# Pooled attention with a gated-convolution FFN on one core: the schedule rewritten, with q in 96 rows, exp in token order and crossbar transposes from batch 2 on

## The chip, the core and the metric

The kernel runs on one core of one Trainium2 chip. The metric is the time of one execution on the device, in microseconds (us). Before the change the median of three runs is 202.54 us (201.12 to 206.23).

## The reference

Eight batches of attention over pooled keys feed an FFN with a gated convolution. Inputs and output are fp32; the kernel computes in bf16 with fp32 sums.

```python
# q, k, v: 8 batches x 8 heads x 576 tokens x 64
k_p = k.reshape(B, H, 72, 8, D).mean(axis=3)         # 576 keys -> 72
v_p = v.reshape(B, H, 72, 8, D).mean(axis=3)
attn = softmax(q @ k_p.T / 8) @ v_p
x = attn.transpose(0, 2, 1, 3).reshape(B, 576, 512)  # tokens x (heads * 64)
h = relu(x @ w_in)                                   # 512 -> 1024
conv_out[s] = sum_k conv_w[k] * h[s + k - 1]         # 3 taps along the tokens, per channel
out = (h * sigmoid(conv_out)) @ w_out                # 1024 -> 512
```

## The kernel before

All five engines work on one program, whose operations are listed with `pl.add` (name, engine or choice of engines, a planned duration, a function that issues it, what it reads and writes). `Planner.order` (L172) turns the list into one order: a list simulation over planned durations, in which `PARAMS["prio"]` breaks ties; `PARAMS["act"]` says which of the operations that could go to DVE or ACT go to ACT. PSUM is cut into three slots of two banks (A) and two of one bank (B). Where the simulation sees PE idle in the first 60 us, `warm` (L379) puts in filler matmuls of 128 columns of zeros (L388).

Attention goes batch by batch, one or two batches ahead of the FFN.

- *Loads.* POOL issues them and casts fp32 to bf16: k (L447, L451) and v (L467 to L479) as 576 rows of eight tokens, w_in in one DMA of 1 MB (L485), w_out in two (L492). q of batches 0 to 4 comes as 72 rows of eight tokens, all heads (L424); q of batches 5 to 7 token by token in five DMAs a batch, whose pieces are the 64 values of one token and head (L412). `PARAMS["rg"]`, "DDDDDTTT", chooses. POOL also makes the scaled identities for the convolution (L571).
- *Keys and values.* DVE adds the eight tokens of each row (L605, L612, L622, and L654 for v). The key sums are transposed on PE and copied into kz (L642), the value sums are spread into blocks (L658, L663).
- *q.* For batches 0 to 4 a copy brings the heads of a token side by side (`regroup`, L432), PE transposes them (L688) and DVE or ACT copies the result to qT (L694). For batches 5 to 7 SP's queue transposes q by DMA, in the crossbar (L676).
- *Scores and values.* L717 and L719 multiply with the keys (the rest of 16 keys of each pair of heads goes through four strips of 32 columns of the array, L719). One exp on ACT covers 128 keys and 576 tokens (L725); it reads and writes rows of 576 without gaps. L742 and L746 multiply with the values, DVE divides by the sum (L755, L759). Batches 0 to 4 carry the tokens of a tile in the order of q's rows, eight apart.
- *x.* For batches 0 to 4 PE transposes each tile of 128 tokens with a permutation in place of the identity, which puts the tokens in order (L779), and a copy takes it to xT (L785). For batches 5 to 7 SP's queue transposes it (L772).
- *FFN.* w_in times xT (L822; for batch 0 in parts of 384 and 192 tokens, L799), relu on ACT (L828, L806). The convolution is either three matmuls with scaled identities on PE (L945) with the gate on ACT out of PSUM (L952), or off PE: two scaled copies on ACT (L868) or DVE (L870), two additions on DVE (L877, L887), and the gate on ACT (L895). A gate is Tanh, which DVE finishes (L923), or Sigmoid, according to `PARAMS["sw"]`; each change between the two, and back to exp, loads a table on ACT. DVE multiplies h by the gate (L933). w_out takes two batches at a time in nine tiles of 128 tokens (L976), a copy on ACT or DVE takes the result out (L999), and SP's queue stores it (L1004) from three buffers.

Of the kernel before, what the change touches and what calls it, by code (L numbers as in the profile page):

```python
# [15 lines left out]
    "prio": (  # L17
# [84 lines left out]


TINY = 1e-20


class Op:
    __slots__ = ("i", "name", "eng", "dur", "lat", "deps", "prio", "fn", "take", "give", "dma", "width", "done", "users", "after", "kind", "unit", "mode")


class Planner:

# [59 lines left out]
    def order(self):  # L172
# [4 lines left out]
        for o in ops:  # L177
# [3 lines left out]
            for d in o.deps:  # L181
                ops[d].users.append(o.i)
# [919 lines left out]
```

## Time and profile before

| | |
|---|---|
| runs of the kernel (us) | 202.54 median, 201.12 to 206.23 |
| profiled execution, its span (us) | 205.9 |
| instructions | 4566 |
| PE busy, at its end a matmul of L976 | 194.9 us |
| the group with most time on PE | L976, 282 matmuls, 65.4 us |
| the next | L822, 448 matmuls, 60.0 us |
| moved by DMA | 30.02 MB in 52330 packets |

The profiled execution is one execution, on the long side of the three runs; its span is counted from the first instruction to the last. An engine's busy time says nothing of when it was busy, so the page's row of forty slices (busy tenths) and a table of busy time by windows stand beside it. Fillers count as busy PE time. A row such as "L725 ACT ACTIVATE attnT<-psfA x40: 628/657/701, 14.7 to 155.9" gives line, engine, tiles, count, least, median and greatest time of one in ns, and when the first and the last ran. In a row by distance from start to start ("99.04 1.72 ACT ...") the first number is the start and the second the time of one instruction or of a run of like ones. A DMA row gives its KB and the median from issue to landing.

### The profile page before, as it was taken

How to read it: one execution, taken by the hardware profiler on the slowest of the kernel's cores; microseconds unless marked ns; L12 is line 12 of the kernel's file. 1: busy time of each engine (PE TensorE's matmuls, PEld its weight loads, DVE VectorE, ACT ScalarE, POOL GpSimd, SP SyncE). 2: the span in 40 equal slices, each digit the busy share in tenths (PEclk: the TensorE clock that was granted, in tenths of full speed). 3: DMA queues.
4: the chain of work that ended last, by engine and by line, in shares of the span. 5: the costliest groups of instructions: out<-in, count | busy, mean ns of one | idle time of the engine just before them, and what ended most of it. 6: DMA issues, size and time to landing. Idle time of an engine off the chain costs nothing.

```text
span 205.9 us, 4566 instructions
## 1 busy us (share of the span) xinstructions
PE 194.9 (95%) x1770; PEld 133.0 (65%) x1770; DVE 173.3 (84%) x396; ACT 165.3 (80%) x275; POOL 57.0 (28%) x90
## 2 busy tenths in 40 slices
PE   6999999999999999999999999669999999999992
PEld 6978775977557776567755775226756765765541
DVE  3598599999999999999999996893897999778522
ACT  2045799999999999999999999494899867979610
POOL 7999497160223276215412000000000000000000
PEclk9999999999999999999999999996999999999999
DMA  3999999999999999999999999772122625004334
GB/s 32 192 202 205 196 200 200 201 184 192 157 193 238 171 125 173 181 147 158 193 137 167 152 103 151 115 203 105 20 57 41 229 78 155 13 0 168 126 117 154
DMA packets 52330, 30.02 MB, mean 146 GB/s; under 512 B 33468, under 2 KB 47316, under 8 KB 52308
## 3 DMA queue, kind: packets, MB, share of 16 engines
q0 software_dynamic: 32384, 16.73, 71.8%
q1 hardware_dynamic: 19924, 12.99, 30.5%
q8 instruction: 14, 0.23, 0.6%
q14 instruction: 8, 0.07, 0.2%
HBM read 33.44 MB, written 9.44 MB: 208 GB/s over the span
## 4 chain that ended last, share of the span: by engine, by line
PE 38%; DMA 26%; ACT 16%; DVE 12%; issue 3%; POOL 3%; SPq 0%; POOLq 0%; DVEq 0%; ACTq 0%
PE psfB L976 14%; DMA v_b<-in_v_dram 13%; PE psfA L822 12%; DMA q_b<-in_q_dram 6%; DMA qT<-q 6%; ACT tg L895 4%; PE pswA L388 3%; ACT attnT L725 3%; PE psfA L742 2%; ACT hT L828 2%; ACT cv L868 2%; PE psfA L945 2%; DVE p L605 2%; DVE cv L870 1%; DMA xT<-xx 1%
## 5 line engine op out<-in xcount | busy, mean ns | idle before, releaser
L976 PE MATMUL psfB<-w_out,gT 128*128 128x512 bf16 (+1 forms) x282 | 65.4, 378 | 0.0
L822 PE MATMUL psfA<-xT,w_in 128*128 128x288 bf16 x448 | 60.0, 291 | 2.2 <-DMA xT<-xx 2.2
L822 PEld LDWEIGHTS <-w_in 128*128 128x128 bf16 x448 | 43.9, 100 | 16.2 <-DMA xT<-xx 2.4
L976 PEld LDWEIGHTS <-gT 128*128 128x128 bf16 x290 | 27.3, 98 | 28.9
L828 ACT ACTIVATE hT<-psfA 128x576 bf16<-128x576 f32 x56 | 35.1, 656 | 8.4 <-PE psfA L822 8.2
L870 DVE TENSOR_SCALAR cv<-hT,cr 128x576 bf16<-128x576 bf16 x75 | 26.3, 378 | 5.6 <-ACT hT L828 5.4
L933 DVE TENSOR_TENSOR gT<-tg,hT 128x1152 bf16<-128x1152 bf16 x32 | 23.6, 749 | 3.9 <-ACT tg L895 2.0
L759 DVE TENSOR_TENSOR xx<-psfA,rr 128x512 bf16<-128x512 f32 (+1 forms) x40 | 26.5, 679 | 0.2
L868 ACT ACTIVATE cv<-hT,cr 128x576 bf16<-128x576 bf16 x33 | 25.1, 776 | 0.4 <-DVE cv L887 0.2
L725 ACT ACTIVATE attnT<-psfA 128x576 bf16<-128x576 f32 x40 | 24.5, 661 | 0.7 <-PE psfA L717 0.5
L895 ACT ACTIVATE tg<-cv,cn 128x576 bf16<-128x576 bf16 x30 | 22.5, 780 | 0.0
L877 DVE TENSOR_TENSOR cv<-cv,hT 128x1152 bf16<-128x1152 bf16 (+1 forms) x31 | 20.9, 676 | 0.3
L887 DVE TENSOR_TENSOR cv<-cv 128x1152 bf16<-128x1152 bf16 (+1 forms) x31 | 20.8, 674 | 0.2
L999 ACT COPY osb<-psfB 128x512 f32<-128x512 f32 x24 | 14.1, 587 | 6.4 <-PE psfB L976 6.3
L412 POOL DMA_DIRECT2D q<-in_q_dram x15 | 12.8, 863 | 20.1 <-DMA qT<-q 11.3
L895 ACT ACTIVATE tg<-cv,cs 128x576 bf16<-128x576 bf16 x24 | 18.2, 772 | 0.2
L388 PEld LDWEIGHTS <-zero 128*128 128x128 bf16 x239 | 16.1, 108 | 2.8 <-DVE zero L497 2.0
L742 PE MATMUL psfA<-vblk,attnT 128*128 128x130 bf16 (+1 forms) x160 | 15.6, 222 | 2.1 <-DVE xx L759 2.0
L742 PEld LDWEIGHTS <-attnT 128*128 128x128 bf16 (+1 forms) x160 | 11.1, 100 | 5.7 <-DVE xx L759 2.9
L388 PE MATMUL pswA<-zero 128*128 128x128 bf16 x150 | 11.5, 249 | 2.0 <-DVE zero L497 2.0
L717 PE MATMUL psfA<-qT,kz 128*128 128x512 bf16 x64 | 12.4, 286 | 0.3
L746 PE MATMUL psfA<-vblk,attnT 128*128 128x130 bf16 (+1 forms) x80 | 11.2, 221 | 0.0
(92 smaller groups left out, 256.6 us busy)
## 6 DMA issues: line engine op xcount, KB each, us to landing
out_dram<-osb SPq DMA_DIRECT2D x14, 512.0 KB, 4.2
k_b<-in_k_dram POOLq DMA_DIRECT2D x8, 512.0 KB, 13.5
v_b<-in_v_dram POOLq DMA_DIRECT2D x7, 512.0 KB, 13.0
q_b<-in_q_dram POOLq DMA_DIRECT2D x4, 576.0 KB, 15.6
out_dram<-osb SPq DMA_DIRECT2D x7, 256.0 KB, 2.2
q<-in_q_dram POOLq DMA_DIRECT2D x12, 128.0 KB, 15.9
w_in<-in_moe_w_in_dram POOLq DMA_DIRECT2D x1, 1024.0 KB, 10.4
w_out<-in_moe_w_out_dram POOLq DMA_DIRECT2D x2, 512.0 KB, 12.5
```

What stands on the lines that cost most here:

```text
L388: nc.tensor.matmul(out=t, lhsT=zero[:, 0:P], rhs=zero[:, 0:P], start=True, stop=True)
L725: nc.scalar.activation(out=attnT[m][:, t, :], in_=slot(key).rearrange("p i x -> p (i x)")[:, 0:S], func=ACT.Exp, scale=1.0 / 64.0)
L742: nc.tensor.matmul(out=a[0:n, g, c * w:(c + 2) * w], lhsT=attnT[m][:, s, u0:u0 + n], rhs=vblk[m][:, 2 * s:2 * s + 2, :].rearrange("p x d - ...
L759: nc.vector.tensor_tensor(out=xx[i3][0:n].rearrange("p (g h e) -> p g h e", g=2, h=4), in0=av_view()[:, :, :, 0:D], in1=rr[i3][0:n].rearra ...
L822: nc.tensor.matmul(out=t[:, i, 0:HC], lhsT=w_in[:, c, f * P:(f + 1) * P], rhs=xT[m][:, c, i * HC:(i + 1) * HC], start=(c == 0), stop=(c == ...
L828: nc.scalar.activation(out=h_(b)[:, f, hs(b), 2:S + 2].rearrange("p (i x) -> p i x", i=2), in_=slot(key)[:, :, 0:HC], func=ACT.Relu)
L868: nc.scalar.activation(out=cv[y][:, kk // 2, z0:z1, :], in_=src, func=ACT.Copy, scale=sc)
L870: nc.vector.tensor_scalar(out=cv[y][:, kk // 2, z0:z1, :], in0=src, scalar1=sc, scalar2=None, op0=OP.mult)
L877: nc.vector.tensor_tensor(out=cv[y][:, 0, 0:n, :], in0=cv[y][:, 0, 0:n, :], in1=h_at(2), op=OP.add)
L895: nc.scalar.activation(out=tg[i3][:, zs[z0]:zs[z0] + z1 - z0, :], in_=cv[y][:, 0, z0:z1, :], func=ACT.Tanh if half else ACT.Sigmoid, scale ...
L933: nc.vector.tensor_tensor(out=o_, in0=tg[i3], in1=h2, op=OP.mult)
L976: nc.tensor.matmul(out=a[:, 0, j0:j1], lhsT=g[:, c, t * P:(t + 1) * P], rhs=w_out[:, c, j0:j1], start=(c == 0), stop=(c == n_fb - 1), skip ...
```

## The change

The kernel is written anew around the same computation. What differs:

- *Order.* The planner's simulation is gone. `PARAMS["order"]` lists all operations in their order, with the PSUM slot of each and the number of fillers ahead of it ("36A0/77@B0": 36 fillers in A0, then operation 77 into B0). 159 fillers are left of 239, nine of them behind the first matmul with w_in.
- *q.* All batches come as 96 rows of six tokens (pieces of 384 values); batch 0 in parts of 64 and 32 rows. For batches 0 to 5 PE transposes each head by itself, straight from the loaded rows, two heads into the two halves of the output's rows; there is no regroup. Batches 6 and 7 are regrouped and go through the crossbar in two DMAs each.
- *exp.* It writes tokens in order, and to do so it reads PSUM in steps of 96 values. The permutation matrices go; L664 transposes x with the plain identity.
- *x.* 27 of 40 tiles go through the crossbar (batch 2's tiles 2 to 4, batch 3's 1 to 4, all of batches 4 to 7), 13 through PE.
- *w_in.* Half of its rows of its first 512 columns come as fp32 words on SP's queue into a buffer and are converted on ACT (`wc2.0` and `wc2.1`); the other half, and the columns from 512, come in two DMAs by POOL. In POOL's order both stand behind q of batch 1.
- *Pooling* adds in place; for v of batch 5 eight matmuls with the identity do it on PE.
- *Placement.* The scaled identities move from POOL to ACT (13) and DVE (5). Scaled copies: 42 on ACT, 66 on DVE. Ten units of the convolution are on PE (batch 0's f 0 to 3, 5 and 7; one of batch 1, two of batch 2, one of batch 4), the others off it. All gates are Tanh. All output copies are on ACT.

The core of the diff (the new kernel's lines are named by its own numbers in the text):

```diff
 def load_q(b, prio):                                  # after: L245, L250
-    nc.gpsimd.dma_start(out=q_rows(b % NQ)[0:n, t].rearrange("p (h d) -> p h d", d=D), in_=q[b, :, P * t:P * t + n].rearrange("h p d -> p h d"))
...
-    nc.gpsimd.dma_start(out=q_b[b % NQ][r0:r1].rearrange("p h i d -> p h (i d)"), in_=rows_q(b)[r0:r1])
+    nc.gpsimd.dma_start(out=q_b[b % NQ], in_=q[b].rearrange("h (p i) d -> p h (i d)", i=TQ))
...
 def attn_q(b):                                        # after: L550, L557, L571
-    nc.tensor.transpose(out=t[:, 0, (j - j0) * PR:(j - j0 + 1) * PR], in_=q2[b % NQ][0:PR, i, 2 * c:2 * c + 2, :].rearrange("p h d -> p (h d)"),
-                        identity=ident[0:PR, 0:PR])
+    i, c = divmod(8 * g + j, CH)
+    for z in range(2):
+        nc.tensor.transpose(out=t[64 * z:64 * z + 64, 0, j * PQ:(j + 1) * PQ], in_=q_b[b % NQ][:, 2 * c + z, i * D:(i + 1) * D], identity=ident[0:PQ, 0:PQ])
...
+    nc.sync.dma_start(out=flat_out[:, 1152 * j:1152 * j + 1152].rearrange("p (g r) -> p g r", r=PQ), in_=flat_in[:, 1536 * j:1536 * j + 1536], transpose=True)
...
 def attn_s(b, t):                                     # after: L607, L615
-    nc.scalar.activation(out=attnT[m][:, t, :], in_=slot(key).rearrange("p i x -> p (i x)")[:, 0:S], func=ACT.Exp, scale=1.0 / 64.0)
+    nc.scalar.activation(out=at(m)[:, t, :].rearrange("p (r i j) -> p r i j", i=2, j=3),
+                         in_=slot(key)[:, :, 0:HC].rearrange("p i (j r) -> p r i j", j=3), func=ACT.Exp, scale=1.0 / 64.0)
...
 def attn_av(b, t):                                    # after: L664, L668, L673
-    nc.tensor.transpose(out=a[:, 0, c * P:c * P + n], in_=xx[i3][0:n, c * P:(c + 1) * P], identity=(ident[0:n, 0:n] if tr else perm4 if last else perm))
+    nc.tensor.transpose(out=a[:, 0, c * P:(c + 1) * P], in_=xx[i3][:, c * P:(c + 1) * P], identity=ident)
...
 def weights_in():                                     # after: L295, L299, L306, L311
-    nc.gpsimd.dma_start(out=w_in, in_=moe_w_in.rearrange("(c p) f -> p c f", p=P))
+    nc.sync.dma_start(out=wf[:, 0:c1], in_=src[:, 0:c1, 0:512])
+    copy_on(e)(out=w_in[:, c, 0:512], in_=wf[:, c, :])
+    nc.gpsimd.dma_start(out=w_in[:, 2:4, 0:512], in_=src[:, 2:4, 0:512])
+    nc.gpsimd.dma_start(out=w_in[:, :, 512:1024], in_=src[:, :, 512:1024])
...
 def attn_v(b):                                        # after: L434, batch 5 alone
+    nc.tensor.matmul(out=view(), lhsT=ident, rhs=src[:, :, i * D:(i + 1) * D], start=i == 0, stop=i == 7)
...
 def consts():                                         # after: L389, L391
-    nc.gpsimd.tensor_scalar(out=dw[f][:, kk, :], in0=ident, scalar1=s, scalar2=1.0, op0=OP.mult, op1=OP.mult)
+    nc.scalar.activation(out=dw[f][:, kk, :], in_=ident, func=ACT.Copy, scale=s)      # or DVE
```

More of the change, by code (lines that the diff above doesn't have):

```diff
@@ L136, in add @@
         o.eng = eng if isinstance(eng, dict) else {eng: dur}
-        if len(o.eng) > 1 and self.on_act is not None:
-            e = "ACT" if name in self.on_act else "DVE"
-            o.eng = {e: o.eng[e]}
-        o.lat = lat
-        o.fn, o.prio, o.take, o.give, o.dma = fn, prio + self.shift.get(name, 0.0), take, give, dma and dma[:2]
-        o.width = dma[2] if dma and len(dma) > 2 else 4
+        o.lat, o.fn, o.take, o.give, o.dma, o.tile = lat, fn, take, give, dma, tile
         deps = set()
@@ L286, in packets @@
-def packets(n, nbytes, cast=True, engines=16):
-    return n / engines, 0.003 + 0.0000785 * nbytes if cast else 0.004 + 0.000034 * nbytes, engines // 4
+        out, seen = [], set()
+        for x in PARAMS["order"].split():
+            warm = None
+            if "/" in x:
+                w, x = x.split("/")
+                warm = (int(w[:-2]), w[-2:])
+            mode = x.endswith("s")
+            x, _, slot = x.rstrip("s").partition("@")
+            o = self.ops[int(x)]
+            o.mode = mode
+            assert o.i not in seen and seen.issuperset(o.deps) and (o.after is None or o.after in seen), o.name
+            seen.add(o.i)
+            if slot:
+                self.held[o.take] = (slot[0], int(slot[1]))
+            e = next(iter(o.eng)) if len(o.eng) == 1 else "ACT" if o.name in self.on_act else "DVE"
+            out.append((e, o, warm))
@@ L430, in regroup @@
+    def regroup(b, x):
         for h in range(0, H, 4):
             def fn(e, h=h):
-                copy_on(e)(out=q2[b % NQ][0:PR, :, h:h + 4, :], in_=q_b[b % NQ][:, h:h + 4].rearrange("p h i d -> p i h d"))
-            pl.add(f"qg.{b}.{h}", {"DVE": 0.6, "ACT": 1.8}, 0, fn, reads=[("ql", b % NQ, 0), ("ql", b % NQ, 1)],
-                   writes=[("q", b % NQ, h + z) for z in range(4)] + ([("qt", b % NQ)] if h else []), prio=pr + 0.01 * h,
-                   free=[("qn", b % NQ, t) for t in range(NT)])
@@ new lines, in load_v, with fn @@
+        if b == 0:
+            for c in range(4):
+                def fn(e, c=c):
+                    nc.gpsimd.dma_start(out=v_b[m][32 * c + 16:32 * c + 32, 4, :], in_=src[P:P + 16, c, :])
+                pl.add(f"ldv{b}.t{c}", "POOL", 0.5, fn, reads=[("vz", m)], writes=[("v", m, 2 + c)], dma=(16, 0.087, 16))
+            return
+        def fn(e):
+            nc.gpsimd.dma_start(out=v_b[m][:, 4, :], in_=src[P - 16:P + 16, :, :].rearrange("y c e -> c y e"))
+        pl.add(f"ldv{b}.t", "POOL", 0.7, fn, reads=[("vz", m)], writes=[("v", m, 2 + c) for c in range(4)], dma=(P, 0.087, 4))
@@ L518, in consts @@
-        pl.add("perm1", "DVE", 0.15, fn, reads=["ident"], writes=[("perm", 1)], prio=-47)
-        def fn(e):
-            t = slot(("cw",))
-            nc.tensor.transpose(out=t[:, 0, 0:24], in_=cw_raw, identity=identf)
-        pl.add("cwT", "PE", 0.1, fn, reads=["cwr", "identf"], writes=["cwp"], prio=-46, take=("cw",))
+            nc.tensor.transpose(out=slot(("cw",))[:, 0, 0:24], in_=cw_raw, identity=identf)
+        pl.add("cwT", "PE", 0.1, fn, reads=["cwr", "identf"], writes=["cwp"], take=("cw",), tile=3)
@@ new lines, in by_identity, with view, fn, attn_k @@
+    def by_identity(b, x, src, reads):
+        key = ("pm", b, x)
+        def view():
+            return slot(key)[:, 0, 0:NT * D].rearrange("p (t d) -> p t d", d=D)
+        def fn(e):
+            for i in range(8):
+                nc.tensor.matmul(out=view(), lhsT=ident, rhs=src[:, :, i * D:(i + 1) * D], start=i == 0, stop=i == 7)
+        pl.add(f"pm{x}.{b}", "PE", 1.09, fn, reads=reads + ["ident"], writes=[key], take=key)
+        return key, view
+    def attn_k(b):
+        m = b % 2
+        src = k_b[m]
+        keys = [("k", m, 0), ("k", m, 1), ("kz", m)]
+        sh = [P, NT, 2, D]
+        def on_dve():
+            pool8(b, "k", src, keys)
+            def fn(e):
+                nc.vector.tensor_tensor(out=ksum, in0=src[:, :, 0:D].unsqueeze(2).to_broadcast(sh), in1=src[:, :, D:2 * D].unsqueeze(2).to_broadcast(sh), op=OP.add)
+            pl.add(f"ksum.{b}", "DVE", 0.40, fn, reads=[("kp", m), *keys], writes=["ksum"])
+        def on_pe():
+            pm, view = by_identity(b, "k", src, keys)
+            def fn(e):
+                copy_on(e)(out=ksum, in_=view().unsqueeze(2).to_broadcast(sh))
+            pl.add(f"ksumP.{b}", {"ACT": 0.59, "DVE": 0.74}, 0, fn, reads=[pm], writes=["ksum"], give=pm)
+        pl.variants(f"k{b}", [on_dve, on_pe])
@@ L633, in fn @@
             t = slot(key, True)
-            for i in range(4):
+            for i in range(NT):
                 nc.tensor.transpose(out=t[:, 0, i * P:(i + 1) * P], in_=ksum[:, i].rearrange("p i d -> p (i d)"), identity=ident)
-            nc.tensor.transpose(out=t[:, 0, 512:576], in_=ksum[0:64, 4].rearrange("p i d -> p (i d)"), identity=ident[0:64, 0:64])
-        pl.add(f"kT.{b}", "PE", 0.29, fn, reads=["ksum", "ident"], writes=[("kTp", b)], prio=pr, take=key, free=[("kz", m, 0), ("kz", m, 1)])
-        kzi = [None]
+        pl.add(f"kT.{b}", "PE", 0.29, fn, reads=["ksum", "ident"], writes=[("kTp", b)], take=key, free=[("kz", m, 0), ("kz", m, 1)])
+        kzi = None
         for x in range(2):
@@ L701, in attn_s, with fn @@
         cs_ = (t,) if t < 4 else (0, 1, 2, 3)
-        tr = PARAMS["rg"][b] == "T"
-        gs = range(5) if tr else sorted({g for g, (j0, j1) in enumerate(QG[b == 0]) for c in cs_ if j0 < 8 * c + 8 and j1 > 8 * c})
+        if b == 0:
+            for x, (r0, r1) in enumerate(QR):
+                key = ("sc0", b, t, x)
+                n = TQ * (r1 - r0)
+                def fn(e, key=key, r0=r0, r1=r1, n=n):
+                    a = slot(key)
+                    for c in cs_:
+                        if t < 4:
+                            nc.tensor.matmul(out=a[:, 0, 0:n], lhsT=kz[m][:, CW * c:CW * c + P], rhs=qT[m][:, :, c, r0:r1], start=True, stop=True)
+                        else:
+                            nc.tensor.matmul(out=a[32 * c:32 * c + 32, 0, 0:n], lhsT=kz[m][:, CW * c + P - 16:CW * c + P + 16], rhs=qT[m][:, :, c, r0:r1],
+                                             start=True, stop=True, tile_position=(0, 32 * c))
+                pl.add(f"sc.{b}.{t}.{x}", "PE", n / 2400 + 0.01, fn, reads=[("kz", m, 0), ("kz", m, 1)] + [("qT", m, i, x) for i in range(TQ)],
+                       writes=[("scp", b, t, x)], take=key, free=[("at", m, t, x)], tile=0 if t < 4 else 1)
+                def fn(e, key=key, r0=r0, r1=r1, n=n):
+                    nc.scalar.activation(out=at(m)[:, t, TQ * r0:TQ * r1].rearrange("p (r j) -> p r j", j=TQ),
+                                         in_=slot(key)[:, 0, 0:n].rearrange("p (j r) -> p r j", j=TQ), func=ACT.Exp, scale=1.0 / 64.0)
+                pl.add(f"exp.{b}.{t}.{x}", "ACT", 0.055 + n / 1200, fn, kind="exp", reads=[("scp", b, t, x)], writes=[("at", m, t, x)], give=key)
+            return
@@ L728, with attn_av @@
+        pl.add(f"exp.{b}.{t}", "ACT", 0.535, fn, kind="exp", reads=[("scp", b, t)], writes=[("at", m, t, 0), ("at", m, t, 1)], give=key)
     avs = [None]
-    def attn_av(b, t, pr):
+    def attn_av(b, t):
         m = b % 2
@@ L780, in attn_av @@
-        pl.add(f"xt.{b}.{t}", "PE", 0.14 if last else 0.222, fn, reads=[("xx", i3), ("perm", 0), ("perm", 1)], writes=[("xtp", b, t)],
-               prio=pr + 0.3, take=key2, free=[("xT", m, t)])
-        def fn(e):
-            w = 64 if last else P
-            copy_on(e)(out=xT[m][:, :, 128 * t:128 * t + w],
-                       in_=slot(key2)[:, 0, 0:512].rearrange("p (c a) -> p c a", c=4)[:, :, 0:w])
-        pl.add(f"xte.{b}.{t}", {"ACT": 0.48, "DVE": 0.335} if not last else {"ACT": 0.265, "DVE": 0.205}, 0, fn, reads=[("xtp", b, t)], writes=[("xT", m, t)],
-               prio=pr + 0.3, give=key2)
@@ L812, in mm1, with hkeys, fn @@
-    def mm1(b, f, pr):
-        if b == 0:
-            return mm1_parts(b, f, pr)
-        m = b % 2
+            pl.add(f"xD.{b}.{t}", "SP", 1.2, fn, reads=[("xx", i3)], writes=[("xT", m, t)], dma=(4 * n, 0.0275, 16))
+        pl.variants(f"x{b}.{t}", [by_matmul, by_crossbar])
+    def hkeys(us):
+        return [("hT", b % 2, f, x) for b, f in us for x in (0, 1)]
+    def mm1(b, f):
+        m = b % 2
+        if b == 0:
+            for x, (j0, j1, ts) in enumerate([(0, 384, (0, 1, 2)), (384, 576, (3, 4))]):
+                key = ("h0", b, f, x)
+                n = j1 - j0
+                def fn(e, key=key, n=n, j0=j0, j1=j1):
+                    t = slot(key)
+                    for c in range(n_dc):
+                        nc.tensor.matmul(out=t[:, 0, 0:n], lhsT=w_in[:, c, f * P:(f + 1) * P], rhs=xT[m][:, c, j0:j1],
+                                         start=(c == 0), stop=(c == n_dc - 1))
+                pl.add(f"mm1.{b}.{f}.{x}", "PE", 4 * n / 2400 + 0.01, fn, reads=[("xT", m, t) for t in ts] + [("wi", f // 4, c) for c in range(n_dc)],
+                       writes=[("hp", b, f, x)], take=key)
+                def fn(e, key=key, n=n, j0=j0, j1=j1):
+                    nc.scalar.activation(out=hT[m][:, f, 2 + j0:2 + j1], in_=slot(key)[:, 0, 0:n], func=ACT.Relu)
+                pl.add(f"relu.{b}.{f}.{x}", "ACT", 0.055 + n / 1200, fn, reads=[("hp", b, f, x)], writes=[("hT", m, f, x)], give=key)
+            return
@@ L883, in fn @@
+        pl.add(f"ca0{x}.{b}.{f}", "DVE", 0.07 + 0.3 * n, fn,
+               reads=[("cv", y, 0, z) for z in cz] + hkeys(us), writes=[("cv", y, 0, z) for z in cz])
         def fn(e):
[L884 to L889 removed]
@@ L890, in conv_off @@
-        gi = {}
-        for z0, z1 in runs:
-            def fn(e, z0=z0, z1=z1):
-                g = us[z0][1]
-                half = not pl.ops[gi[z0]].mode
-                nc.scalar.activation(out=tg[i3][:, zs[z0]:zs[z0] + z1 - z0, :], in_=cv[y][:, 0, z0:z1, :],
-                                     func=ACT.Tanh if half else ACT.Sigmoid, scale=cs[:, g:g + 1] if half else cn[:, 1, g:g + 1])
-            gates.append((zs[z0], zs[z0] + z1 - z0, pl.add(f"tanh.{b}.{us[z0][1]}", "ACT", 0.185 + 0.48 * (z1 - z0), fn, kind="gate",
-                   unit=(n_tg[0], 0.5 * (z1 - z0)), reads=[("cv", y, 0, z) for z in range(z0, z1)] + ["cs"],
-                   writes=[("tg", i3, zs[z]) for z in range(z0, z1)], prio=pr)))
-            gi[z0] = gates[-1][2]
@@ L938, in conv_pe, with fn @@
-    def conv_pe(b, f, i3, z, pr, gates):
+            nc.vector.tensor_tensor(out=cv[y][:, 0, 0:n, :], in0=cv[y][:, 0, 0:n, :], in1=cv[y][:, 1, 0:n, :], op=OP.add)
+        pl.add(f"ca2{x}.{b}.{f}", "DVE", 0.07 + 0.3 * n, fn,
+               reads=[("cv", y, k2, z) for k2 in (0, 2) for z in cz], writes=[("cv", y, 0, z) for z in cz])
+        gi = {}
+        for z in range(n):
+            def fn(e, z=z):
+                half = not pl.ops[gi[z]].mode
+                nc.scalar.activation(out=tg[i3][:, z, :], in_=cv[y][:, 0, z, :], func=ACT.Tanh if half else ACT.Sigmoid,
+                                     scale=cs[:, f + z:f + z + 1] if half else cn[:, 1, f + z:f + z + 1])
+            gi[z] = pl.add(f"tanh{x}.{b}.{f + z}", "ACT", 0.665, fn, kind="gate", unit=(n_tg[0], 0.5), reads=[("cv", y, 0, z), "cs"], writes=[("tg", i3, z)])
+            gates.append((z, gi[z]))
```

818 lines of the change are left out of this document (293 added, 525 removed), and 111 rows, old and new, of the table PARAMS.

## The prediction

> **What bounds the kernel now.** I read the page's first parts, then the table by stage, then the chain of waits where the table shows a hole.
>
> ```profile
> span 205.9 us, 4566 instructions
> PE 194.9 (95%) x1770; PEld 133.0 (65%) x1770; DVE 173.3 (84%) x396; ACT 165.3 (80%) x275; POOL 57.0 (28%) x90
> PE   6999999999999999999999999669999999999992
> DMA  3999999999999999999999999772122625004334
> ```
>
> PE looks full at 95%, but the busy time holds filler matmuls (L388, 128 columns of zeros). The table by stage and the fillers' own rows part them:
>
> ```profile
> 12.00:22.00 10.00, 9.67 (x161) 8.05 (x159) 9.09 (x25) 5.81 (x11) 9.58 (x21) 1.00 1.19 204
> 22.00:44.00 22.00, 21.38 (x276) 16.61 (x274) 19.59 (x47) 20.21 (x39) 12.14 (x18) 1.00 1.26 197
> 44.00:128.00 84.00, 83.83 (x747) 56.47 (x744) 81.50 (x188) 82.82 (x138) 24.86 (x32) 1.00 1.59 166
> 128.00:146.00 18.00, 13.79 (x98) 8.03 (x97) 12.66 (x29) 11.60 (x21) 0.00 (x0) 0.91 0.55 126
> 146.00:194.00 48.00, 48.00 (x339) 30.38 (x337) 40.77 (x85) 42.10 (x67) 0.00 (x0) 1.00 0.29 86
> 194.00:205.90 11.90, 8.23 (x41) 3.72 (x38) 3.16 (x5) 1.24 (x3) 0.00 (x0) 0.96 0.42 156
> ...
> 22.00:44.00 22.00, 3.89 (x53) 2.99 (x50) 1.00 1.26 197
> ```
>
> (Columns: window, length, then PE, PEld, DVE, ACT, POOL; granted clock, DMA share, GB/s. The last row is L388 alone: PE and PEld only.) Up to 22 us PE waits for the first loads. From 22 to 44 it fills 3.89 us while DVE and ACT carry batch 0's gates and batch 1's attention. From 44 to 128 all three engines are full. From 128 to 146 there is a hole. From 146 on PE alone is full. So the bound is PE, less four places where it does no work of use: the lead, 22 to 44, the hole, and the tail. The hole, in the chain of waits and PE's timeline:
>
> ```profile
> 108.03 21.40 DMA v_b<-in_v_dram
> 129.53 0.83 DVE p L605
> 136.45 2.72 DMA xT<-xx
> 139.22 6.62 PE psfA L822 x39
> ...
> 140.00:146.00 6.00, 6.00 (x41) 4.30 (x39) 3.18 (x8) 3.39 (x6) 0.00 (x0) 0.72 0.24 88
> ...
> 173.75 8.00 PE L822 MATMUL psfA<-xT,w_in 128*128 128x288 bf16 x64
> 181.59 1.89 PE L976 MATMUL psfB<-w_out,gT 128*128 128x512 bf16 x8
> ```
>
> A load of v takes 21.4 us, DVE stands, PE idles, and then 39 matmuls at a granted clock of 0.72 take 6.62 us. At the price of 173.75 to 181.59 (7.84 / 64 = 0.1225) they are 4.78. Hole: 18.00 - 13.79 = 4.2 idle, and 1.8 slow, together 6.0 us.
>
> **The change part by part.**
>
> ```profile
> qT<-q SPq DMA_TRANSPOSE x15, 10.9
> xT<-xx SPq DMA_TRANSPOSE x15, 2.5
> w_in<-in_moe_w_in_dram POOLq DMA_DIRECT2D x1, 1024.0 KB, 10.4
> DMA packets 52330, 30.02 MB, mean 146 GB/s; under 512 B 33468, under 2 KB 47316, under 8 KB 52308
> L772 SPq DMA_TRANSPOSE xT<-xx x15: 1170/1216/2101, 124.1 to 171.4; - x15
> L725 ACT ACTIVATE attnT<-psfA x40: 628/657/701, 14.7 to 155.9; 128x576 bf16<-128x576 f32 x40
> ```
>
> *Token loads go.* q of batches 5 to 7 came in 15 DMAs of one 64-value row per token and head: 3 x 4608 = 13,824 of the 33,468 small packets. It now comes in 3 DMAs of 768 rows of 384 values. These DMAs stood in POOL's queue around the v load that is late, and the DMA share of 1.59 at only 166 GB/s is theirs (1.26 at 197 before). With 2,304 packets in their place I take the hole as gone: **-6.0**. Ends: -6.0, and 0 if v was late for its buffer alone. Late next is whichever xT comes last by crossbar.
>
> *Filler stage.* The new order puts batch 0's gates mostly on PE (f 0 to 3, 5 and 7, against 1, 4 and 5 before) and batch 2's scores ahead of batch 1's first matmuls. Nine fillers are left behind the first matmul of the FFN, against 53: 9/53 of 3.89 is 0.7. **-3.2**. Ends: -3.9, and 0 if the new gaps are merely not filled. I stay near the first, as DVE, full there, gets less work (below).
>
> *PE's own work.* Out go 12 tiles' transposes (4 matmuls, about 0.22 each, -2.7). In come batch 5's q transposes (+1.0) and the sum over v of batch 5 by identity, 8 x 320 columns at 0.1225/288 (+1.1). q is now turned in pairs of 64 columns of the array, which I price as overlapping:
>
> ```profile
> 133.66 0.67 PE L719 MATMUL psfA<-qT,kz 128*32 128x512 bf16 x16
> 134.27 0.42 PE L717 MATMUL psfA<-qT,kz 128*128 128x512 bf16 x2
> ```
>
> Those 16 matmuls (8 of 512 columns, 8 of 64, in four strips) took 0.61 us where in a row they would take 1.96. If pairs don't overlap, each of five batches costs 1.0 more: +5.0 as the upper end. Batch 1's q transposes (1.1) also move ahead of the first FFN matmul, under the wait for loads. Together **-1.7**.
>
> *First FFN matmul (22.2 us).* A quarter of w_in now comes as 32-bit words on SP's queue (0.52 MB instead of 0.26), the rest in two DMAs behind q of batch 1 (0.59 MB), which stood behind w_in before. At 204 GB/s that is 4.2 us more data ahead of it. Against it, the words move in the first microseconds, when the DMA row shows 3, and ACT now converts them. No row prices this. Ends 0 and +3.5; I take **+1.5**, nearer 0, since PE does q's transposes meanwhile. Exp in parts (64 rows, then 32) and the missing regroup of q bring the first scores, but v sets av: no gain.
>
> *ACT and DVE.* ACT by distance from start to start:
>
> ```profile
> 97.71 1.44 ACT L868 ACTIVATE cv<-hT,cr 128x576 bf16<-128x576 bf16 x2
> 99.04 1.72 ACT L828 ACTIVATE hT<-psfA 128x576 bf16<-128x576 f32 x3
> 104.36 0.62 ACT L999 COPY osb<-psfB 128x512 f32<-128x512 f32 x1
> 104.83 1.49 ACT L895 ACTIVATE tg<-cv,cn 128x576 bf16<-128x576 bf16 x2
> 108.74 1.28 ACT L725 ACT_TABLE_LOAD   x1
> ...
> L806 ACT ACTIVATE hT<-psfA 128x384 bf16<-128x384 f32 x5 | 2.5, 492 | 0.4 <-PE psfA L799 0.2
> L806 ACT ACTIVATE hT<-psfB 128x192 bf16<-128x192 f32 x5 | 1.7, 335 | 0.0
> L432 ACT COPY q<-q_b 72x2048 bf16<-72x2048 bf16 x2 | 3.8, 1894 | 0.0
> L694 ACT COPY qT<-psbB 128x792 bf16<-128x792 bf16 x4 | 3.3, 814 | 0.0
> L642 ACT COPY kz<-psbB 64x288 bf16<-64x288 bf16 x8 | 3.2, 397 | 7.5 <-PE psbB L636 7.4
> L785 ACT COPY xT<-psbB 128x512 bf16<-128x512 bf16 x10 | 5.7, 585 | 3.0 <-PE psbB L779 2.9
> ```
>
> Scaled copies go from 33 to 42 (x 0.665: +6.0), output copies from 25 to 37 (x 0.47: +5.6), q copies from 8 to 16 (0.81 less the 0.1 of overlap: +5.6), kz from 9 to 12 (+1.1), 13 scaled identities of 128 columns (about 0.3, from the slope 492 to 335: +3.9), w_in and v copies (+1.3). Out go both regroups (-3.6), four xT copies (-1.9) and five table loads (-6.4), as every gate is now Tanh. Sum +11.6: ACT 165.3 to 177.
>
> DVE:
>
> ```profile
> L999 DVE COPY osb<-psfB 128x512 f32<-128x512 f32 x10 | 6.9, 687 | 3.1 <-PE psfB L976 3.1
> L432 DVE COPY q<-q_b 72x2048 bf16<-72x2048 bf16 x8 | 5.9, 752 | 0.8 <-DMA q_b<-in_q_dram 0.8
> L923 DVE TENSOR_SCALAR tg<-tg 128x1152 bf16<-128x1152 bf16 x11 | 4.9, 446 | 0.4 <-ACT tg L895 0.4
> ```
>
> It loses 12 output copies (-8), four of eight regroups and a quarter of the rest (-4), and the q, xT, scaled and v work that went to ACT, SP or PE (about -10); it gains Tanh's fix-up on all 32 units (+7.5). About 173 to 159, so it is no bound. Moved to ACT, the work lies beside PE, which costs nothing while ACT has idle time: the windows leave ACT 14.7 us idle up to 22 and 10.7 after 194. About 6 us of the new work fills the first, so ACT alone needs 177 + 8.7 + 10.7 = 196.4. It has no slack left, and each microsecond more on ACT is a microsecond.
>
> *Crossbar.* From batch 2 on, 27 tiles of x and 4 half q's are turned by SP. A tile costs 1.22 at SP and 2.5 to landing, where PE and a copy took about 1.0. What covers it is attention's lead: the last exp starts at 155.9, the last batch's first FFN matmul at 173.75. Cost 0; if the lead is gone, each late batch pays like the hole's end, 2.2 idle and 1.8 slow, 4.0. Queued behind a waiting transpose on SP are the output stores, and behind those the three output buffers.
>
> *Sum.* 205.9 - 6.0 - 3.2 - 1.7 + 1.5 = 196.5, and ACT's own bound says 196.4. That is against the profiled execution's span. The median of the runs, 202.54, is 3.4 below it. Part of that I put down to a smaller hole, which is gone in both; I keep 1.5 of it. **Predicted: 195.0 us.**
>
> **The rivals.**
>
> *1. Crossbar waits in the place of the hole.* For it: in this trace PE's one wait for xT is a crossbar transpose, and those of q took 10.9 us beside loads. Against: xT's median is 2.5. Two late batches give 195 + 8 = 203; four or more, 211.
>
> *2. ACT's exp reads PSUM in steps (slower).* To write tokens in order, exp at L615 of the new kernel reads single f32 values 96 apart, where L725 reads a row of 576. From 492 and 335 ns the price is 0.82 ns a value, 0.47 us for 576. If each value costs double, 40 exps cost 18.8 us, ACT has no slack, and the time is 195 + 18.8 = 213.8. It is slower than before by over 2% from 0.29 us an exp on. Against: the strided copy L432 takes 1894 ns for 2048 values, 0.92 each with its fixed part, no more than a plain one; but its runs are 64 long and in SBUF. The Trainium skill, "Advanced Engine Details and Errata", section "PSUM Cachelines", says lines of PSUM hold two f32 values and that steps slow matmuls; by it, carried over to ACT, this rival holds. No run here shows it yet.
>
> *3. The weights are late.* First FFN matmul at +3.5, with PE idle long enough to lose the clock as after the hole (1.8): 195 + 2 + 1.8 = 198.8.
>
> **How the numbers follow.** A measurement of this kernel can tell 2% from no change: below 198.5 is faster, above 206.6 slower. Forecast 0.62 (187 to 198.5: lower end all terms at their good end, -6.0 - 3.9 - 2.7 + 0, and ACT's tail 4 shorter); two late batches 0.12; four or more 0.05; exp 0.11; weights 0.10. Faster 0.62, same 0.22, slower 0.16. The range from 187 to 205 leaves out 0.16.
>
> **What would show it.** Right: no hole in PE's row after 44, the clock at 1.00 throughout, ACT at about 177 busy and full from 25 to 185, exp rows near 660 ns, pairs of q overlapping, xT landing in 2.5 to 4 us. Wrong: PE waiting for DMA xT, exp rows above 0.9 us, v again 20 us on the way, or the first FFN matmul after 26.

## The result

The changed kernel is slower: 219.94 us median of 4 runs (217.12 to 220.93) against 203.77 of the kernel before on the same chip; ratio 1.0795, 95% interval 1.0629 to 1.0961. The forecast of 195.0 and its range up to 205 are both missed. The profiled execution has a span of 215.4 us. Medians, here and below, are of all runs; ratios and their intervals leave out the runs in a second, slower state that a program falls into now and then.

The page of the changed kernel, its first parts:

```profile
span 215.4 us, 4647 instructions
PE 194.3 (90%) x1826; PEld 132.6 (62%) x1826; DVE 160.4 (74%) x367; ACT 175.9 (82%) x317; POOL 37.9 (18%) x66
PE   6898999999999399993999909999999999999993
PEclk9799999999999969999699985999999999999999
DMA  5999999999953997199977792495245066214074
```

PE's busy time is that of before (194.9), but its row has three notches, and behind each the granted clock falls to 0.5 or 0.6. By stage (columns as in the prediction):

```profile
22.00:44.00 22.00, 21.70 (x298) 17.01 (x298) 14.20 (x36) 20.89 (x50) 7.33 (x13) 1.00 1.28 201
44.00:140.00 96.00, 83.03 (x760) 56.33 (x758) 74.39 (x168) 77.02 (x132) 14.05 (x19) 0.93 0.88 142
140.00:200.00 60.00, 59.93 (x428) 37.90 (x426) 56.68 (x124) 59.60 (x101) 0.00 (x0) 1.00 0.45 118
```

From 44 to 140 PE stands still for 13 us and DVE and ACT for some 20 each. From 140 on, PE and ACT are full and the clock is whole. So the loss lies between 44 and 140. What ended PE's gaps there (PE's timeline; the gap and its releaser are in the brackets), and the group of these matmuls:

```profile
72.05 0.30 PE L705 MATMUL psfA<-xT,w_in 128*128 128x288 bf16 x1 [0.57 <-DMA xT<-xx]
75.85 3.68 PE L705 MATMUL psfA<-xT,w_in 128*128 128x288 bf16 x15 [3.50 <-DMA xT<-xx]
99.03 0.30 PE L705 MATMUL psfA<-xT,w_in 128*128 128x288 bf16 x1 [0.81 <-DMA xT<-xx]
101.89 2.52 PE L705 MATMUL psfA<-xT,w_in 128*128 128x288 bf16 x15 [2.56 <-DMA xT<-xx]
129.37 1.86 PE L705 MATMUL psfA<-xT,w_in 128*128 128x288 bf16 x7 [5.33 <-DMA xT<-xx]
...
L705 PE MATMUL psfA<-xT,w_in 128*128 128x288 bf16 x448 | 65.9, 301 | 12.8 <-DMA xT<-xx 12.8
```

All 12.8 us of waiting are for x from the crossbar, at the first matmuls of batches 2, 3 and 4 (64 of these matmuls belong to a batch, from batch 1 on). The chain of waits names the transposes, and POOL's timeline shows what was issued beside them:

```profile
69.14 6.66 DMA xT<-xx
93.57 8.27 DMA xT<-xx
120.48 8.84 DMA xT<-xx
...
68.35 0.54 POOL L268 DMA_DIRECT2D k_b<-in_k_dram  x1 [19.86 <-DVE cv L729]
...
72.76 0.78 POOL L264 DMA_DIRECT2D k_b<-in_k_dram  x1
92.89 1.44 POOL L287 DMA_DIRECT2D v_b<-in_v_dram  x2 [19.35 <-DVE vs L496]
...
119.56 0.72 POOL L287 DMA_DIRECT2D v_b<-in_v_dram  x1 [22.34 <-PE psfA L607]
120.28 1.78 POOL L276 DMA_DIRECT2D v_b<-in_v_dram  x2
```

POOL stands for about 20 us at a load whose buffer is not free (the tail, the last and smaller load, of batch 6's keys, then of batch 6's and batch 7's values) and lets everything behind it go at once: seven loads from 68.35, six from 92.89, three from 119.56. Each burst meets the transposes that PE waits for next, the last tile of each batch (64 tokens). It lands in 6.66 to 8.84 us, where the first tile of batch 2, at 66.4, took 2.5.

### The profile page after: what moved, and what is told of

The parts are those of the page before. It is cut to its first block, busy times and chain, and to the rows that moved or that the text cites. A ratio compares the mean times of both kernels' runs of the same rounds, so it can differ in the third digit from the quotient of the medians.

```text
span 215.4 us, 4647 instructions
## 1 busy us (share of the span) xinstructions
PE 194.3 (90%) x1826; PEld 132.6 (62%) x1826; DVE 160.4 (74%) x367; ACT 175.9 (82%) x317; POOL 37.9 (18%) x66
## 4 chain that ended last, share of the span: by engine, by line
PE 42%; DMA 22%; ACT 16%; DVE 11%; POOL 4%; issue 2%; ACTq 0%; DVEq 0%; POOLq 0%
PE psfA L705 18%; PE psfB L818 14%; DMA xT<-xx 11%; DMA v_b<-in_v_dram 7%; ACT tg L746 5%; DMA k_b<-in_k_dram 4%; ACT hT L711 3%; PE psfA L633 3%; ACT cv L727 2%; ACT attnT L615 2%; DVE gT L796 2%; DVE cv L739 2%; PE psfA L637 1%; ACT qT L557 1%; DVE cv L734 1%
## 5 line engine op out<-in xcount | busy, mean ns | idle before, releaser
L705 PE MATMUL psfA<-xT,w_in 128*128 128x288 bf16 x448 | 65.9, 301 | 12.8 <-DMA xT<-xx 12.8
L746 ACT ACTIVATE tg<-cv,cs 128x576 bf16<-128x576 bf16 x54 | 40.7, 788 | 0.6 <-DVE cv L739 0.4
L727 ACT ACTIVATE cv<-hT,cr 128x576 bf16<-128x576 bf16 x42 | 32.8, 797 | 0.1
L650 DVE TENSOR_TENSOR xx<-psfA,rr 128x512 bf16<-128x512 f32 x40 | 27.2, 686 | 3.1 <-DMA xT<-xx 2.4
L646 DVE RECIPROCAL rr<-psfA 128x8 f32<-128x8 f32 x40 | 7.8, 200 | 18.8 <-PE psfA L637 18.6
L841 ACT COPY osb<-psfB 128x512 f32<-128x512 f32 x33 | 19.5, 598 | 2.6 <-issue 1.1
L790 DVE TENSOR_SCALAR tg<-tg 128x1152 bf16<-128x1152 bf16 x32 | 14.6, 461 | 4.4 <-ACT tg L746 4.3
L633 PE MATMUL psfA<-vblk,attnT 128*128 128x130 bf16 x160 | 16.5, 227 | 0.8 <-ACT attnT L596 0.5
L633 PEld LDWEIGHTS <-attnT 128*128 128x128 bf16 x160 | 12.6, 102 | 5.6 <-issue 0.7
L419 DVE TENSOR_TENSOR k_b<-k_b 128x1280 bf16<-128x1280 bf16 x8 | 6.6, 820 | 10.7 <-DMA k_b<-in_k_dram 10.7
L226 PEld LDWEIGHTS <-zero 128*128 128x128 bf16 x159 | 12.3, 119 | 1.3 <-DVE zero L323 1.1
## 6 DMA issues: line engine op xcount, KB each, us to landing
v_b<-in_v_dram POOLq DMA_DIRECT2D x7, 512.0 KB, 12.8
```

The lines of the kernel that those rows point to most:

```text
L226: nc.tensor.matmul(out=t, lhsT=zero[:, 0:P], rhs=zero[:, 0:P], start=True, stop=True)
L633: nc.tensor.matmul(out=a[:, g, c * w:(c + 2) * w], lhsT=attnT[m][:, S * s + u0:S * s + u0 + P], rhs=vblk[m][:, 2 * s:2 * s + 2, :].rearran ...
L650: nc.vector.tensor_tensor(out=xx[i3].rearrange("p (g h e) -> p g h e", g=2, h=4), in0=av_view()[:, :, :, 0:D], in1=rr[i3].rearrange("p (g ...
L705: nc.tensor.matmul(out=t[:, i, 0:HC], lhsT=w_in[:, c, f * P:(f + 1) * P], rhs=xT[m][:, c, i * HC:(i + 1) * HC], start=(c == 0), stop=(c == ...
L727: nc.scalar.activation(out=cv[y][:, kk // 2, z, :], in_=src, func=ACT.Copy, scale=sc)
L746: nc.scalar.activation(out=tg[i3][:, z, :], in_=cv[y][:, 0, z, :], func=ACT.Tanh if half else ACT.Sigmoid, scale=cs[:, f + z:f + z + 1] if ...
```

## The experiments

Theory T (traffic): loads in flight slow the transposes, and the bursts put loads there. Rival R: tiles of x are late by the crossbar or by SP's order, whatever else moves. Rival B: another bound, with the waits in its slack. Spans are of the profiled execution of each run; ratios are to the kernel before on the same chip.

**e1, no late loads.** The late batches compute on rows that an earlier batch left; the order of all other work stays. Waits of DVE for late loads can't be what goes: it waits 10.7 us for k in the changed kernel and 10.9 here.

```diff
 # load_k, load_v, load_q
+            if b >= 5:        # v: 4, q: 6
+                return
```

> The changed kernel without its last loads: k from batch 5, v from batch 4 and q from batch 6 are not loaded, so that the late batches compute on rows that an earlier batch left. Theory T (traffic): the three long waits for xT (12.8 us idle, and 5.9 us by which L705 is slower than before) come from loads that POOL issues in bursts at 68.4, 92.9 and 119.6 us, into which the crossbar transposes fall. Then every transpose of x lands in 2.3 to 3.5 us, PE has no wait of over 1 us behind 60 us, and the span is 215.4 - 12.8 - 5.9 = 197, give or take 2. Rival R (the crossbar or SP's order itself): tiles of x are issued too late or turned too slowly whatever else moves; then the waits stay within a third and the span is over 209.

Measured: 199.75 us, ratio 0.985 (0.973 to 0.996). The page and PE's waits:

```profile
span 197.7 us, 4619 instructions
PE   7798999999999999999999999999999999999991
L715 PE MATMUL psfA<-xT,w_in 128*128 128x288 bf16 x448 | 61.0, 286 | 0.6 <-DMA xT<-xx 0.5
```

The notches are gone. 12.8 - 0.5 = 12.3 us of waiting and 65.9 - 61.0 = 4.9 us of slow matmuls are 17.2, and the spans differ by 215.4 - 197.7 = 17.7. That is nearly all of it: T, not R, and B has half a microsecond of room. It also shows what the rest of the change is worth where nothing collides: about 1.5% (0.4 to 2.7), and that with some of the loads left out.

**e2, x of batches 2 to 5 on PE.**

```diff
-    "x2.2": 1, "x2.3": 1, "x2.4": 1, "x3.1": 1, ... "x5.4": 1
+    # 17 tiles by L664, copies on DVE
```

> The changed kernel with the 17 tiles of x of batches 2 to 5 that went through the crossbar turned on PE again, with a copy on DVE; batches 6 and 7 stay on the crossbar. T and R both: no wait for xT up to 140 us; 197 + 17 x 0.22 us of PE (3.7) = 201 of span, 202 to 203 of time, which is about the kernel before. A third theory, B (ACT or the new order is the bound, and the waits only fill its slack): the time stays over 212.

Measured: 210.03 us, ratio 1.037 (1.028 to 1.046), span 207.0. No wait for xT up to 140 us, but only 8.4 us of span are back where 14 were expected. Against e1 PE is busy 5.5 us longer (194.6 to 189.1; 3.7 was expected), and from 60 to 128 us it idles 4 us in small pieces: PE's queue now holds a transpose where SP's had held it, and waits there for DVE. That the place in PE's order is at fault was not tried.

**e3, another order of the loads.**

```diff
-POOL: k6.tail k5 k5.tail v4.tail v4 q6 k6 | v6.tail v5.tail q7 k7 k7.tail v5 | v7.tail v6 v7
+POOL: k5 k5.tail v4.tail v4 | v5.tail v5 q6 k6 k6.tail | v6.tail v6 q7 k7 k7.tail | v7.tail v7
```

> The changed kernel with the same loads in another order on POOL's queue: k and v of batches 5 and 4 ahead of batch 6's key tail (which waits for batch 4's pooling and holds the queue from 48.5 to 68.4 us), v of batch 5 next, batch 7's q and k behind v of batch 6. Nothing else moves. T: the first burst starts about 14 us earlier for 1.2 of its 2.4 MB, so the transposes of 66 to 69 us land in under 4 us and the wait of 4.1 us there is gone; of the burst at 92.9 and of that at 119.6 less is left. The time falls by 5 to 14 us, to 206 to 215. R: it stays within 2 us of the changed kernel's 219.9.

Measured: 212.61 us, ratio 1.047 (1.038 to 1.057), within the range of T. POOL's and PE's timelines:

```profile
53.92 0.76 POOL L265 DMA_DIRECT2D k_b<-in_k_dram  x1 [7.13 <-DVE cv L730]
116.17 0.73 POOL L288 DMA_DIRECT2D v_b<-in_v_dram  x1 [21.50 <-PE psfA L608]
116.90 0.78 POOL L277 DMA_DIRECT2D v_b<-in_v_dram  x1
...
74.12 3.61 PE L706 MATMUL psfA<-xT,w_in 128*128 128x288 bf16 x15 [2.54 <-DMA xT<-xx]
125.42 1.86 PE L706 MATMUL psfA<-xT,w_in 128*128 128x288 bf16 x7 [3.97 <-DMA xT<-xx]
```

The first loads go 14 us earlier, so the queue's head was what had held them. But the wait at 74 is only shorter, not gone as expected, and batch 3's stays (3.1 us for 3.4). And the two loads at 116 (640 KB) suffice for a wait of 4 us, where the burst of three (1.2 MB) had made 5.3. Batch 4's last transpose lands there in 8.3 us; in e1, behind the same store and no load, in 3.7.

**e4, the kernel before with wide pieces** (its own hole, as the prediction explained it).

```diff
-in_=q[b, :, P * t:P * t + n].rearrange("h p d -> p h d")
+in_=q[b].rearrange("h p d -> (h p d)")[P * t * 512:(P * t + n) * 512].rearrange("(p e) -> p e", e=512)
```

> The kernel before, with its token loads of q (batches 5 to 7) reading the same bytes in pieces of 512 values in place of 64, so that q of these batches is in the wrong order. If the hole from 128 to 146 us came of these small pieces, as the prediction had it: v lands in about 12 us instead of 21, the hole of 4.2 us idle and 1.8 us slow is gone, the time falls by 5 to 6 us. If v was late for its buffer or for the traffic as such: the time falls by under 2 us and a wait stays at 128 us.

Measured: 203.54 us, ratio 1.004 (0.997 to 1.010). Its page:

```profile
span 200.0 us, 4566 instructions
PE   5989999999999999999999999999999999999992
DMA packets 40235, 30.02 MB, mean 150 GB/s; under 512 B 19645, under 2 KB 35221, under 8 KB 40213
```

12,095 packets fewer change nothing that can be measured. This profile has no hole, but the median has not moved either; e7 is the unchanged kernel once more.

**e5, gates.** A copy of one element on POOL reads xT ahead of a load, and the load and all behind it wait until x has landed.

```diff
+    "gate": {'ldk6.t': (2, 4), 'ldv6.t': (3, 4), 'ldv7.t': (5, 1)},
...
+    nc.gpsimd.tensor_copy(out=gate[:, b:b + 1], in_=xT[b % 2][:, 0, P * t:P * t + 1])
```

> The changed kernel with three one-element copies on POOL that read xT, so that the loads behind them wait until x has landed: ahead of batch 6's key tail (waits for batch 2's last tile of x), of batch 6's value tail (batch 3's last tile) and of batch 7's value tail (batch 5's second tile; v of batch 6 goes one place up for it). The loads move 3 to 9 us later, nothing is left out. T (traffic): the transposes that started the three waits (6.7, 8.3 and 8.8 us to landing) land in under 4 us; the holes shrink to what the later k and v cost, at most 2 us each: span 199 to 204, time 201 to 206. R (crossbar or SP's order): span stays over 211. If the loads have no slack, a wait of DVE for k or v takes the place: span over 206 with a hole behind 80 us whose end is a load.

Measured: 223.81 us, ratio 1.097 (1.087 to 1.107). POOL's and PE's timelines:

```profile
72.55 0.66 POOL L900 COPY gate<-xT 128x1 bf16<-128x1 bf16 x1 [24.41 <-DMA xT<-xx]
97.46 0.86 POOL L900 COPY gate<-xT 128x1 bf16<-128x1 bf16 x1 [19.13 <-DMA xT<-xx]
...
114.82 0.59 PE L467 MATMUL psbB<-ident,ksum 128*128 128x128 bf16 x5 [3.32 <-DVE ksum L451]
126.82 1.03 PE L708 MATMUL psfA<-xT,w_in 128*128 128x288 bf16 x7 [0.77 <-DMA xT<-xx]
143.59 1.14 PE L610 MATMUL psfA<-qT,kz 128*128 128x288 bf16 x4 [3.82 <-DMA qT<-q]
148.77 0.59 PE L636 MATMUL psfA<-vblk,attnT 128*128 128x130 bf16 x4 [4.04 <-DVE xx L653]
```

Waits for xT fall from 12.8 to 0.8 us, as T says, and transposes of batches 2 and 3 land in 2.4 to 4.0. But DVE now waits for the loads (4.2 us twice for k, 9.5 for v), and PE behind DVE and q: the new waits cost more than the old. The loads had no slack: the time that I gave, 201 to 206, was wrong, and the third case was nearest. Part of it is the third gate's place. It reads batch 5's second tile (landed at 133.4), but the third hole is batch 4's, whose last tile had landed at 126.8: 6.6 us of the 9.5 for v may be owed to that. A gate on batch 4 was not tried.

**e6, gates and the order of e3.**

> The three gates, and the load order of the run before: k of batch 5 and v of batch 4 ahead of the first gate, v of batch 5, q and k of batch 6 behind it, v of batch 6, q and k of batch 7 behind the second, v of batch 7 behind the third. T: no transpose of x starts beside a load from 60 us on, each lands in under 4 us, no wait for xT over 1 us, the early loads are in time: span 198 to 200, time 200 to 202, 1 to 3 us under the kernel before. R: over 211. If q and k are late instead: 203 to 207.

Measured: 219.6 us, ratio 1.077 (1.070 to 1.083); a miss. DVE's timeline has the reason:

```profile
107.71 0.83 DVE L422 TENSOR_TENSOR k_b<-k_b 128x1280 bf16<-128x1280 bf16 x1 [4.65 <-DMA k_b<-in_k_dram]
142.94 0.82 DVE L422 TENSOR_TENSOR v_b<-v_b 128x1280 bf16<-128x1280 bf16 x1 [10.35 <-DMA v_b<-in_v_dram]
```

k of batch 7 stands fourth in its group and is 4.65 us late; v of batch 7 is held until batch 5's second tile of x has landed (128.2; batch 4's last at 120.3) and is 10.35 late. A gate moves the wait to whoever needs the load that it holds.

**e7, the kernel before once more.**

> The kernel before, a second profile. If the hole from 128 to 146 us is in every execution, its span is 204 to 206 and v's load takes about 21 us again; if it comes and goes with the loads' timing, an execution of about 201 us has none, and the median of the runs (203.0) already has part of the 6.0 us that the prediction took for it.

```profile
span 203.2 us, 4550 instructions
PE psfA L945 <- POOL dw L571: 2.4, 1, 2.4
```

One run, 204.86 us. No wait at 128: the longest is one of 2.4 us for a scaled identity on POOL, from a stage where the first profile had none. The hole of 6.0 us is not in every execution of the kernel. What made it in the first profile stays open: e4 has none with wide pieces, and this run has none with small ones.

**e8 and e9, a third buffer for v, with and without gates.** The buffer lets v be loaded a batch sooner, so three groups of loads can lie between the transposes.

```diff
-    v_b = [st(f"v_b{i}", [P, NT, 512], BF16) for i in range(2)]
+    v_b = [st(f"v_b{i}", [P, NT, 512], BF16) for i in range(3)]
...
+POOL: k5 v4 v5 | gate x2.4: q6 k6 v6 | gate x3.4: k7 q7 v7
```

> v gets a third buffer, so that its loads wait for a pooling one batch older, and the loads go in three groups that lie between the transposes: k of 5, v of 4 and 5 from about 54 us; q, k of 6 and v of 6 behind a gate on batch 2's last tile of x (72 us); k, q and v of 7 behind a gate on batch 3's last tile (92 us), k first, as it came 4.7 us late in the run before. No gate stands ahead of batch 5's tiles. T: every transpose of x up to batch 5 lands in under 4 us and no load is late: PE has no wait of over 1 us behind 60 us, span 198 to 200, time 200 to 202, against about 204 for the kernel before on the same chip. If the work has no room for the loads between the transposes whatever their order, a wait for k, v or q of over 2 us stays and the span is over 203.

> The run before without its two gates: the same buffers and the same order, loads start as soon as their buffer is free. If the order and the third buffer do it alone, the same time as with the gates (within 1 us). If the gates matter: q and k of batch 6 go at about 68 us, beside batch 2's transposes, k and q of batch 7 at 87 us, beside batch 3's, these land in 6 us or more, PE waits 2 to 4 us at each, and the span is 3 to 8 us over that with the gates.

Measured: with gates 208.04 us, ratio 1.028 (1.022 to 1.034); without 220.05, ratio 1.087 (1.079 to 1.096). The same loads in the same order and buffers differ by 11 to 12 us through two copies of one element (12.0 by the medians, 11.3 by the runs behind the ratios). PE's timeline with gates, and its wait for xT without them:

```profile
76.81 4.03 PE L709 MATMUL psfA<-xT,w_in 128*128 128x288 bf16 x16 [4.28 <-DMA xT<-xx]
122.43 1.03 PE L709 MATMUL psfA<-xT,w_in 128*128 128x288 bf16 x7 [0.88 <-DMA xT<-xx]
...
PE psfA L709 <- DMA xT<-xx: 11.5, 5, 6.5
```

With gates one hole is left, at batch 2: there the first group, now with v of batch 5 in it, is still under way (transposes from 67.5 us on land in 6.8 to 8.8).

**e10 and e11, that hole closed in two ways.** e10 moves v of batch 5 behind the first gate; e11 leaves it and turns batch 2's three tiles on PE.

```diff
-POOL: k5 v4 v5 | gate x2.4: q6 k6 v6 | gate x3.4: k7 q7 v7
+POOL: k5 v4 | gate x2.4: q6 k6 v5 v6 | gate x3.4: k7 q7 v7        # e10
+POOL: k5 v4 v5 q6 k6 v6 | gate x3.4: k7 q7 v7, x2.2 to x2.4 on PE  # e11
```

> The run with the third v buffer and two gates, but v of batch 5 (640 KB) moves from the first group of loads, which was still on its way when batch 2's tiles were turned (a wait for xT of 4.3 us at 72.5), to the second, behind the gate. T: that wait goes as well, no wait for xT of over 1 us is left, span 206.3 - 4.3 and some 1.8 of slow clock = 200, time 201 to 203, within 2% of the kernel before. If the second group is now too long (2.4 MB) and runs into batch 3's transposes: a wait of 3 to 5 us at 90 us takes its place and the time stays at 206 to 209.

> The run with the third v buffer, but batch 2's three tiles of x are turned on PE, so that the first group of loads meets no transpose; the gate ahead of q of batch 6 goes, the one on batch 3's last tile stays. T: 206.3 - 6.1 + 3 x 0.22 of PE = 201 of span, time 202 to 204. If the second group, now released at about 68 us, runs longer into other work: up to 206.

Measured: e10 205.94 us, ratio 1.020 (1.014 to 1.027), span 202.9; e11 204.89 us, ratio 1.014 (1.007 to 1.020), span 204.2. PE's waits in e10, and its chain of waits:

```profile
PE psfA L613 <- ACT attnT L619: 3.2, 1, 3.2
PE psfA L709 <- DMA xT<-xx: 1.0, 1, 1.0
...
85.55 7.64 DMA out_dram<-osb
93.21 0.59 ACT osb L845
93.79 0.56 ACT attnT L619
```

The wait for xT at 72 shrinks to 1.0 us, and one of 3.2 opens at 94. It is not for xT: an output store is 7.64 us on its way beside the longer second group, ACT's next output copy waits for the store's buffer, and the exp that PE needs stands behind that copy. Batch 3's transposes take 6.4 to 7.8 us there, and no wait for them is left. In e11 the wait of 2.4 us is for q's transposes (7.28 us on their way). So here traffic reaches PE by other ways than x. Both kernels are 14 to 15 us under the changed one (on other chips), but neither beats the kernel before.

## Why the prediction was wrong

- *Crossbar, the step that failed:* "What covers it is attention's lead [...] Cost 0". The lead was read from the last exp (155.9) to the last batch's first FFN matmul (173.75), 18 us. But the weighted sum, the division and the transpose come between:

```profile
170.16 0.68 DVE L759 TENSOR_TENSOR xx<-psfA,rr 64x512 bf16<-64x512 f32 x1
...
DMA to landing us min/median/max: 2.3/2.5/6.7
```

These are views of the kernel before: its last tile is divided by 170.84, its transpose starts at 171.41 and lands at 173.75, and the first matmul of the batch (by count the one at 174.73) comes 3.9 us after the division. In the changed kernel the last tiles of batches 2, 3 and 4 are divided at 67.66, 92.35 and 119.18 (ends of DVE's L650), and PE stands at their first matmuls 3.8, 5.9 and 4.6 us later. Such a lead covers a landing of 2.5 us; in the bursts it took 6.7 to 8.8. The price was in the trace before twice: q's transposes beside loads took 10.9 us, which I used as an argument for a rival and not as the price, and the longest of x, 6.7, is the first one, at 124.07, while loads still ran. e1 settles the size: 17.7 us, in three holes.
- *What was not followed:* POOL's queue. The change reorders it, and the prediction counted bytes and packets on it, not which load stands at its head and for whom it waits. That made the bursts (e3 shows that loads behind it could have gone 14 us earlier; e8 against e9 that their time, not their amount, sets the cost).
- *Rival 1* was the mechanism, at 0.17 in all. Its price was too low: 4.0 a late batch against 17.7 / 3 = 5.9, because it was worked out from the one wait of the trace before, at a time when the loads were done.
- *The hole, -6.0:* it was in that one execution, and not in every one of the kernel. e4 and e7 have none at 128, and e4's time is that of before: small pieces cost nothing here that can be measured. The profiled execution was 3.4 us over the median, for which 1.5 were kept; the typical run had less of a hole to lose.
- *The rest of the sum* is borne out only as a whole. First matmul with w_in at 25.0 us for 22.2: +2.8 where +1.5 was taken (ends 0 and 3.5). With the other two terms as predicted, 205.9 - 6.0 - 3.2 - 1.7 + 2.8 = 197.8, and e1 has 197.7. The terms -6.0, -3.2 and -1.7 are shown only together, and e1 leaves loads out, so that an agreement to 0.1 us is in part luck. ACT 175.9 (predicted 177), DVE 160.4 (159).
- *Rival 2 (exp in steps) and pairs of q.* The groups of the changed kernel:

```profile
L615 ACT ACTIVATE attnT<-psfA 128x576 bf16<-128x576 f32 x35 | 21.9, 665 | 0.1
L550 PE MATMUL psbB<-ident,q_b 96*64 96x96 bf16 x144 | 4.3, 207 | 0.0
L550 PE MATMUL psbA<-ident,q_b 96*64 96x96 bf16 x96 | 3.1, 208 | 0.0
L389 ACT ACTIVATE dw<-ident,cw 128x128 bf16<-128x128 bf16 x13 | 5.2, 419 | 0.0
```

An exp that reads PSUM in steps of 96 values takes 665 ns in the mean and 670 at the median, where the plain one took 657 at the median: the rival is out, and the Trainium skill's rule on steps in PSUM ("Advanced Engine Details and Errata", section "PSUM Cachelines"), which is written of matmuls, does not carry over to ACT here. Pairs overlap in part: 240 transposes in 4.3 + 3.1 us are 31 ns each, where 96 columns at the prediction's 0.1225 us per 288 would be 41, and two at once 20; the 48 of a batch take 1.5 us. A scaled identity costs 0.42 and not 0.3.
- *How they share:* of the burst at 92.89, the transpose issued at 93.57 met first the value tails of batches 6 and 5:

```profile
v_b<-in_v_dram POOLq DMA_DIRECT2D x7, 128.0 KB, 8.0
```

The tails are small but slow: these two landed at 99.55 and 101.64, the transpose at 101.84 (8.27 us). The Trainium skill, "DMA: Bandwidth & Descriptors", section "Queues, rings and completion order", says that an engine takes turns among the queues that have work, a packet at a time. The trace agrees: in its packet records from 73 to 74 us SP's queue has 152 of 256 bytes (transposes) and POOL's 150 of 1 KB (loads), and from 127 to 128 they have 150 and 151. A transpose's packet took 31 ns there, and 18 from 68 to 68.5, where POOL's queue moved nothing. Whether single packets alternate or longer turns, these counts don't show. Two things come on top. The transpose of 120.48 moved nothing until 126.0, as the output store ahead of it in SP's queue was under way; beside loads that store took 6.3 us, in e1 4.05. And from 95.5 to 98 SP's queue moved next to nothing, while sixteen 4-byte packets of POOL's queue took 3.0 to 3.1 us each; why, no run here shows.
- *Also open:* the rest of e2, and why e10 and e11 stay 5 to 6.5 us of span over e1. Waits of 1 to 3 us each are seen there, and only that of e10 at 94 and that of e11 for q are followed to their causes.

## What to carry to other kernels

Price a transfer by its time in the stage where it will run, beside what else is in flight there, not by its median over the program. Where a queue is reordered, look for the entry at its head that waits, and for what it lets go at once and whom that meets. And where two profiles of one kernel are to be had, look whether the hole is in both before its removal is counted as a gain.

## What the runs showed of the hardware

A crossbar transpose of 128 or 64 x 512 bf16 took 2.3 to 2.6 us to landing alone. In e1, without the late loads, none took over 5.8, and those over 4.0 stood right behind an output store. In the holes, beside loads, it took 6.4 to 8.8, and 14.8 at most (e9, issued at 98.3). A load of 512 KB beside one took 10.6 us (e3, v of batch 7). Behind a stretch in which PE stood idle the granted clock is down for some microseconds: after the 3.5 us of the first hole it is 0.54 for 3.7 us (15 matmuls in 3.68 us) and then 1.00, after the 5.3 us of the third 0.52 for 4.7. In e1, at the place of the first hole, it is 1.00 and they take 2.01:

```profile
71.76 2.01 PE L715 MATMUL psfA<-xT,w_in 128*128 128x288 bf16 x15 [0.15 <-DMA xT<-xx]
```
